# A planned TensorE order: keeping other matmuls out of the way of score groups

## The chip, the core and the metric

The kernel runs on one core of a Trainium2 chip. The metric is the device time of one execution in microseconds. The engines are TensorE (PE in the profile, PEld for its weight loads), VectorE (DVE), ScalarE (ACT), GpSimd (POOL) and SyncE (SP), which issues DMAs. Each works through its own list of instructions in order; semaphores tie the lists together.

## The reference

One transformer block with adaptive layer norm: 2048 tokens, width 640, 32 heads of 20, and a bilinear MLP of width 1536. Everything is bfloat16.

```python
def _A_ref(x, wqkv, wo):
    B, S, D = x.shape                       # 1, 2048, 640
    H = 32; Dh = D // H                     # heads of 20
    qkv = (x @ wqkv).reshape(B, S, 3, H, Dh).transpose(2, 0, 3, 1, 4)
    q, k, v = (qkv[0], qkv[1], qkv[2])
    scores = jnp.einsum('bhqd,bhkd->bhqk', q, k) * Dh ** (-0.5)
    p = _softmax(scores, axis=-1)
    o = jnp.einsum('bhqk,bhkd->bhqd', p, v)
    return o.transpose(0, 2, 1, 3).reshape(B, S, D) @ wo

def _B_ref(x, w_gate, w_up, w_down):
    g = jnp.einsum('bsd,df->bsf', x, w_gate)
    u = jnp.einsum('bsd,df->bsf', x, w_up)
    return jnp.einsum('bsf,fd->bsd', g * u, w_down)

mod = (_silu(c) @ w_mod).reshape(c.shape[0], 6, 1, -1)   # sa, ca, ga, sb, cb, gb
h = _layernorm(x) * (1 + ca) + sa
x = x + ga * _A_ref(h, A_wqkv, A_wo)
h = _layernorm(x) * (1 + cb) + sb
x = x + gb * _B_ref(h, B_w_gate, B_w_up, B_w_down)
```

The scores are 32 x 2048 x 2048 numbers, 134 million exponentials. Most are made by ScalarE's Exp. About a fifth of the score units go to VectorE instead, which makes an exponential out of integer steps (L1267, L1295, L1300 and L1303 below).

## The kernel before

The kernel doesn't write its instructions down in order. It makes tasks with durations and dependencies, and a planner in Python runs a small model of the five engines and decides, for each engine, which ready task comes next. What comes out is a fixed program. The lists of the engines are thus the result of the constants and of the picking rules.

The tensor that matters is `ps_all`, the eight accumulation banks of 512 float32 columns. Banks 0 to 2 and 3 to 4 are the two score buffers A and B, 5, 6 (and 2 at first) take everything else in turn (`G`), bank 7 collects the products with V.

A score group is two units of 128 keys x 512 queries (three in A late in the kernel: 1536 columns). ScalarE turns a group into the probabilities `PP` with one Exp; then its banks are free again. With the exponential of A running, TensorE is to fill B, and the other way round:

```python
    for g, (us, b0) in enumerate(glist):
        bset = setA if b0 == 0 else setB
        # ... ems: the score matmuls (L1209: ps_all<-QT,KT)
        ts = Task("pe", 216.0, ems, list(dict.fromkeys(deps)), ctr="pes", mode="S", name=f"S{g}")
        ts.acq = [(bset, "b", 1)]
        # ...
            ta = Task("act", nu * 512 / 1.2 + 52.0, fexp, [ts], prio=g, name=f"E{g}")   # L1243: PP<-ps_all
            ta.acq = [(pPs[g % 2], "p", nu)]

            def on_e(task, ...):
                bset.done(0, task)      # the exponential gives the score bank back
                sc.progress = max(sc.progress, g + 1)
```

All other TensorE work, projections, transposes, output projection and MLP, stands in "rounds" that take one bank of `G`. A matmul of these and the products with V are cut into quarters: four matmuls of 32 output rows side by side (mode "P"), which together take one step. Score groups are cut by rows (mode "S"), transposes use the whole array (mode "X"). A change of mode is planned as 100 ns:

```python
PE_SWITCH = 100.0
    def mode_start(mode, t):
        s = max(t, sc.pe_end)
        if sc.pe_mode is not None and sc.pe_mode != mode:
            s += PE_SWITCH
        return s
```

When TensorE is free in the model, `pick_pe` chooses. A score group whose bank is free comes first; else V products (`pv_issue`), if enough of them are ready; else the next matmul of a round (`pick_x`); else a filler, a matmul with the identity that only keeps TensorE active, when its activity of late is too low:

```python
    def pick_pe(t):
        sc.pull("pe")
        g = pvstate["sidx"]
        if g < NG:
            ts, us = score_q[g]
            if (...) and acquire_ready(ts, t):
                start = mode_start("S", t)
                rows = {}
                # ...
                d_attach(ts, t, apos[g] + EAGER, rows, 2, False)   # units for VectorE go along
                # ... issue the group
                return True
        # ... units for VectorE that are late
        if sc.recent(t) < FILL_MIN and ring() >= RINGLOW and pick_x(t, True):
            return True
        # ...
        cands = pv_candidates(t, PVCAP)
        it = st_pv["item"]
        if cands:
            info = item_info[it]
            ring_low = ring() < RINGLOW
            ending = info["left"] <= len(cands)
            force = ring_low or ending
            cands = pv_balance(cands, force)
            nwork = sum(1 if k == "a" else 4 for k, _ in cands)
            if cands and (nwork >= (PVMIN if just_s[0] else PVMAX) or force):
                just_s[0] = False
                pv_issue(cands, t)
                return True
        # ...
        if pick_x(t):
            return True
        # ...
        if t > 4000 and fill_ok(t, fill_deps):
            return do_fill(t)
        return False
```

A V product batch can hold up to 16 units, several steps. A filler is one matmul over the whole array (`FILL_MODE = 'X'`, 128x512 from `ident`). How early the rounds of the MLP and of the projections become pickable is set by gates in terms of finished exponentials (`GATE_F`, `K_LEAD`, `WM_NEED` and others).

The units for VectorE: L1267 evicts a unit to `DB` with an add and a maximum, L1295, L1300 and L1303 make two terms of four units in `DSS`, which go into V products as well. Lines of the profile that recur: L773 quarter matmuls of values, output projection and MLP, L888 and L940 those of K and Q, L1689 V products, L1936 fillers.

Of the kernel before, what the change touches and what calls it, by code (L numbers as in the profile page):

```python
# [23 lines left out]
DMA_LAT = 1700.0  # L24
STEAL_END = 85877.564
STEAL_GAP = 300.0
HAM_W = 3413.3
# [3 lines left out]
class Task:  # L31
    __slots__ = ("eng", "dur", "lat", "deps", "emits", "ctr", "prio", "gate", "acq", "on_start", "slots",
                 "start", "done", "needed", "val", "know", "nleft", "ready", "users", "name", "mode", "seq", "rt", "sem",
                 "nbytes", "cond", "alt", "land")

    def __init__(self, eng, dur, emits, deps=(), ctr=None, prio=0.0, lat=None, gate=0, acq=(), on_start=None,
                 name="", mode="X", nbytes=0):
        self.eng = eng
        self.dur = dur
        self.emits = emits if isinstance(emits, list) else [emits]  # L40
        self.deps = [d for d in deps if d is not None]
        self.ctr = ctr or eng
        self.prio = prio
        self.gate = gate
        self.acq = list(acq)
        self.on_start = on_start
        self.slots = {}
        self.start = None
        self.done = None
        self.needed = False  # L50
        self.val = None
        self.know = None
        self.name = name
        self.mode = mode
        self.users = []
        self.nbytes = nbytes
        self.sem = None
        self.cond = None
        self.alt = None
        self.land = 0.0  # L60
        if lat is None:
            lat = {"pe": PE_DRAIN, "act": ACT_LAT, "dve": DVE_LAT, "pool": 60.0}.get(eng, 0.0)
        self.lat = lat
# [50 lines left out]
class Sched:  # L114

    def __init__(self):
# [19 lines left out]
        self.ndup = 0  # L136
        self.nsteal = 0
        self.hist = []
        self.acts = []
        self.left = 0  # L140

    def add(self, task):
# [79 lines left out]
    def step_engine(self, eng):  # L222
# [5 lines left out]
        for k, task in enumerate(rl):  # L228
            if task.gate > self.progress or (task.cond is not None and not task.cond()):
                continue  # L230
            if self.acquire(task, self.t):
                rl.pop(k)
                self.finish_issue(task, self.t, task.dur)
                self.free_at[eng] = self.t + task.dur
                return True
# [168 lines left out]
HEADG = 600  # L404
EAGER = 0
X_POOL, X_PIECES, POOL_NS = 0, 4, 2.2
GU_ONE = 0
# [3 lines left out]
NPS = 4  # L411
TS_4X, TT_2X = 600.0, 1145.0
WM_GATE = 15
WM_NEED = 1.824
K_DIRECT = (0, 1, 2, 3)
Q_DIRECT = 2
K_LEAD = 0.703
K_ALL = (0,)
KD_LEAD = 0.686
DMA_WINDOW = 900000  # L420
D_LATE = 13
D_RES = 75
PVMIN, PVMAX, PVCAP = 2, 13, 16
GATE_F = [0.8, 0.788, 1.0, 0.673, 1.0]
FILL_MIN = 4200.0
FILL_HARD = 0.0
FILL_MODE = 'X'
DUP_MIN = 0.0
XN_POOL = ()
XFIRST = 0  # L430
LN2P = 1.495
NALT = 1
OPFIRST = 0
HT_L = 0.099
V_L = 0.079
LATE_A = 1.127
LATE_L = 3
LATEQ = (3,)
LATEQ_A = 0
LATEQ_F = 0.561  # L440
# [12 lines left out]
def build_kernel(nc, A_x, A_wqkv, A_wo, B_x, B_w_gate, B_w_up, B_w_down, c, w_mod, out):  # L453
# [96 lines left out]

    PPs = [alloc("PP", [128, NPS, w * 512], BF16) for w in (3, 2)]
    wo7 = alloc("wo7", [128, D], BF16)
# [99 lines left out]
    def pool(dur, f, deps=(), prio=3.0, **k):  # L652
        return sc.add(Task("pool", dur, f, deps, prio=prio, **k))

# [165 lines left out]
    def ln1(tc, prio):  # L820
# [3 lines left out]
        for i in range(4):  # L824
            t = tc * 4 + i
            bns = []
            for hf in range(2):
# [13 lines left out]
            if tc in XN_POOL:  # L841
                t_xn[tc].append(pool(1000, f, [p2] + dps, prio=prio + .5))
            else:
                t_xn[tc].append(dve(360, f, [p2] + dps, prio=prio + .05 + .1 * i))

# [344 lines left out]
    for k in range(KD):  # L1190
        t_wo.append(dve(395, lambda e, k=k: e.tensor_tensor(wo_sb[:, k, :], wo_sb[:, k, :], gab[:, 0, :], ALU.mult),
                         d_wo + ev_ga, prio=2.45))
# [3 lines left out]
    for f_ in range(FT):  # L1196
        t_wd.append(dve(395, lambda e, f_=f_: e.tensor_tensor(wd_sb[:, f_, :], wd_sb[:, f_, :], gab[:, 1, :],
                                                                ALU.mult), [d_wd] + ev_gb, prio=2.45))
# [19 lines left out]
    st_pv = {"item": 0, "free": [d_pz]}  # L1218
    d_state = {}
    for qi, (it, us) in enumerate(dquads):  # L1220
        d_state[qi] = {"units": us, "p1": [None] * 4, "slot": None, "item": it}
        for x, u in enumerate(us):
            u.quad = (qi, x)
# [50 lines left out]
    for qi, (it, us) in enumerate(dquads):  # L1274
# [3 lines left out]
        def term(f, deps, dur, name, slot=None, src=None, last=False, it=it, qi=qi, st_=st_):  # L1278
            t = Task("dve", dur, f, deps, prio=2.5 + .001 * qi, name=f"{name}.{qi}")
            if slot is not None:  # L1280
                t.acq = [(sSS, "s", 1)]
            t.cond = lambda: it <= st_pv["item"]

            def on_t(task):
                if slot is not None:
                    st_["ss"][slot] = task.slots["s"]
                if last:
                    sB0.done(st_["slot"], task)
# [16 lines left out]
        tm = term(fm, list(st_["p1"]), TS_4X, "M", slot=0)  # L1305
        if X_POOL and qi % X_POOL == 0:
            deps = [tm]
            for x in range(X_PIECES):
                w = 2048 // X_PIECES

                def fxp(e, x=x, w=w, st_=st_):
                    d = DSS[:, st_["ss"][0], x * w:x * w + w].bitcast(BF16)
                    return e.tensor_tensor(d, DB0[:, st_["slot"], x * w:x * w + w].bitcast(BF16), d, ALU.mult)
                t = Task("pool", w * POOL_NS + 150.0, fxp, deps, prio=.1 * qi, name=f"XP.{qi}")

                def on_p(task, x=x, st_=st_):
                    if x == X_PIECES - 1:
                        sB0.done(st_["slot"], task)
                        st_["src"][0] = [task]
                t.on_start = on_p  # L1320
                sc.add(t)
                deps = [t]
        else:
            term(fx, [tm], TT_2X, "X", src=0, last=True)
        term(fe, list(st_["p1"]), TS_4X, "EX", slot=1, src=1, last=True)

# [33 lines left out]
    def item_end_tasks(it):  # L1360
# [15 lines left out]
        else:  # L1376
            t3 = dve(sb_cost(n, 1.04), f3, [t2], prio=1.5)
        t4 = dve(n * 1.1 + 65, lambda e: e.transpose(OcT[:, cell["s"], 0:n], OTn[:, 0:n]), [t3], prio=1.5)  # L1378
# [32 lines left out]
    def suffix(ci):  # L1411
# [30 lines left out]
        for tl in range(ntl):  # L1442
# [21 lines left out]
            for hf in range(2):  # L1464
# [6 lines left out]
                      [p1], prio=1)  # L1471
            t_xn2.append(dve(360, lambda e, t=t, tl=tl: e.tensor_scalar(
                xn2[:, tl, :], xck[:, tl, :], mv2[:, t, 0:1], rs2[:, t:t + 1], op0=ALU.subtract, op1=ALU.mult),
# [153 lines left out]
    def mode_start(mode, t):  # L1627
        s = max(t, sc.pe_end)
        if sc.pe_mode is not None and sc.pe_mode != mode:
            s += PE_SWITCH  # L1630
        return s

# [204 lines left out]
    def pick_pe(t):  # L1837
# [44 lines left out]
        elif not tail_added[0]:  # L1882
# [6 lines left out]
            else:  # L1889
                tail_added[0] = False  # L1890
        if sc.recent(t) < FILL_MIN and ring() >= RINGLOW and pick_x(t, True):
            return True
# [9 lines left out]
        if cands:  # L1902
            info = item_info[it]
            ring_low = ring() < RINGLOW
            ending = info["left"] <= len(cands)
            force = ring_low or ending
            cands = pv_balance(cands, force)
            nwork = sum(1 if k == "a" else 4 for k, _ in cands)
# [102 lines left out]
```

The softmax here doesn't subtract the row's maximum and nothing guards it: scores larger than these inputs give would overflow.

## Time and profile before

| | before |
|---|---|
| time, median of 3 runs (lowest to highest) | 839.69 us (839.03 to 841.29) |
| span of the profiled execution | 836.0 us |
| TensorE clock granted, mean | 0.996 |
| Exp on ScalarE (L1243) | 778 instructions, 765.0 us |
| score matmuls (L1209) | 2560 instructions |
| VectorE score units (L1267) | 404 instructions, 267.0 us |
| fillers (L1936) | 119 instructions, 42.7 us |
| POOL busy | 78.5 us |

The span is what the profiler saw from first to last instruction. The record of a group of instructions reads: line, engine, operation, output from input, shapes, count, then busy time, mean length of one, idle time of the engine just ahead of them and what ended most of it. Two things need care. The end of a matmul is modelled, so a step of 216 ns shows as 385. And the records of consecutive exponentials overlap, so busy time says less than the distance between starts. In all text, a step is one pass of 512 columns through the array: four quarter matmuls or one whole one.

### The profile page before, as it was taken

To read this page: it belongs to the slowest core of one execution; us is meant where nothing else is said; L and a number is where in the kernel's file an instruction comes from. 1 tells how busy PE (TensorE), PEld (TensorE's weight loads), DVE (VectorE), ACT (ScalarE), POOL (GpSimd) and SP (SyncE) were. 2 spreads that over 40 slices of the span, in tenths; PEclk is the share of its full clock that TensorE was granted. 3 is DMA by queue.
4 is the path that set the end of the run, shared out by engine and by line. 5 is a ranking of instruction groups with operands and counts; after the bars stand their busy time and mean duration, and the time that the engine had idled before them with its cause. 6 is when DMAs were issued, how large, how long until landed. Compare 5 with 4: busy or idle time off the path is not lost.

```text
span 836.0 us, 28503 instructions
## 1 busy us (share of the span) xinstructions
PE 807.9 (97%) x12313; PEld 305.5 (37%) x12313; DVE 732.2 (88%) x1286; ACT 780.7 (93%) x809; POOL 78.5 (9%) x104
## 2 busy tenths in 40 slices
PE   8999999999999999999999999999999999999998
PEld 4433333222232222233232222332244433454577
DVE  7988999999799999998999999998789978757673
ACT  4899999999999999999999999999999999999921
POOL 2310000000011000000021000000011000001000
PEclk9999999999999999999999999999999999999999
DMA  9263411134200235000300221001200226106330
GB/s 301 74 192 88 95 43 43 49 98 126 58 18 20 58 79 160 2 15 20 92 2 13 53 60 39 13 22 40 53 4 22 53 60 130 45 29 141 84 82 20
DMA packets 115899, 54.29 MB, mean 65 GB/s; under 512 B 83771, under 2 KB 115775, under 8 KB 115775
## 3 DMA queue, kind: packets, MB, share of 16 engines
q1 hardware_dynamic: 114847, 51.33, 24.2%
q8 instruction: 97, 1.59, 0.8%
q10 hardware_dynamic: 928, 1.15, 0.4%
q14 instruction: 27, 0.22, 0.1%
HBM read 41.75 MB, written 8.41 MB: 60 GB/s over the span
## 4 chain that ended last, share of the span: by engine, by line
PE 63%; DVE 18%; ACT 13%; issue 5%; POOL 1%; DVEq 0%; ACTq 0%
PE ps_all L773 21%; PE ps_all L1209 20%; PE ps_all L1689 14%; ACT PP L1243 13%; DVE DB L1267 6%; PE ps_all L940 4%; DVE DSS L1300 2%; DVE DSS L1303 2%; DVE st L828 1%; PE ps_all L888 1%; DVE DSS L1295 1%; DVE OT L1366 1%; PE ps_all L1936 1%; POOL OTn L1371 1%; DVE OcT L1378 1%
## 5 line engine op out<-in xcount | busy, mean ns | idle before, releaser
L1243 ACT ACTIVATE PP<-ps_all 128x1024 bf16<-128x1024 f32 (+1 forms) x778 | 765.0, 1104 | 6.2 <-PE ps_all L1209 4.3
L1209 PE MATMUL ps_all<-QT,KT 32*128 32x512 bf16 (+1 forms) x2560 | 319.7, 340 | 12.4 <-ACT PP L1243 7.8
L1267 DVE TENSOR_SCALAR DB<-ps_all 128x512 int16<-128x512 f32 x404 | 267.0, 680 | 42.9 <-PE ps_all L1209 41.4
L1209 PEld LDWEIGHTS ps_all<-QT,KT 32*128 32x128 bf16 x2560 | 84.8, 91 | 264.1 <-ACT PP L1243 192.8
L1689 PE MATMUL ps_all<-PP,Vf 128*32 128x512 bf16 (+3 forms) x2076 | 161.5, 343 | 0.5 <-DVE OT L1366 0.4
L1300 DVE TENSOR_TENSOR DSS<-DB,DSS 128x2048 bf16<-128x2048 bf16 x101 | 122.0, 1208 | 0.0
L773 PE MATMUL ps_all<-h2T,stg 128*32 128x512 bf16 x1440 | 114.3, 386 | 1.2 <-DVE DB L1267 1.0
L1371 POOL TENSOR_TENSOR OTn<-OT,invT 128x512 bf16<-128x512 f32 (+1 forms) x39 | 48.0, 1232 | 612.3 <-DVE invT L1369 612.3
L1689 PE MATMUL ps_all<-DSS,Vf 128*32 128x512 bf16 (+1 forms) x968 | 79.6, 349 | 1.1 <-DVE DSS L1300 0.5
L1689 PEld LDWEIGHTS ps_all<-PP,Vf 128*32 128x32 bf16 (+1 forms) x2076 | 46.2, 94 | 86.1 <-issue 78.7
L1303 DVE TENSOR_SCALAR DSS<-DB 128x2048 int16<-128x2048 int16 x101 | 71.9, 712 | 0.0
L1295 DVE TENSOR_SCALAR DSS<-DB 128x2048 int16<-128x2048 int16 x101 | 69.4, 687 | 0.9
L773 PE MATMUL ps_all<-wd,hprod 128*32 128x320 bf16 x1152 | 57.9, 301 | 0.2 <-DVE DB L1267 0.2
L773 PEld LDWEIGHTS ps_all<-h2T,stg 128*32 128x32 bf16 x1440 | 31.7, 95 | 37.0 <-issue 20.5
L1936 PE MATMUL ps_all<-ident 128*128 128x512 bf16 x119 | 42.7, 409 | 1.9 <-POOL ident L729 1.5
L1558 DVE CAST gsb<-ps_all 128x512 bf16<-128x512 f32 (+1 forms) x48 | 29.5, 614 | 7.5 <-PE ps_all L773 7.2
L773 PE MATMUL ps_all<-wo,Ocp 128*32 128x320 bf16 x640 | 34.0, 301 | 0.9 <-DVE OcT L1378 0.5
L1689 PEld LDWEIGHTS ps_all<-DSS,Vf 128*32 128x32 bf16 x968 | 24.5, 95 | 27.4 <-issue 11.9
L773 PEld LDWEIGHTS ps_all<-wd,hprod 128*32 128x32 bf16 x1152 | 27.5, 96 | 17.8 <-issue 8.5
L773 PE MATMUL ps_all<-wV,hT 128*32 128x320 bf16 x640 | 31.5, 301 | 0.1
L1366 DVE STREAM_TRANSPOSE OT<-ps_all 128x512 f32<-128x512 f32 (+1 forms) x40 | 24.1, 603 | 7.6 <-PE ps_all L1689 7.5
L940 PE MATMUL ps_all<-hT,wq 128*32 128x512 bf16 x375 | 30.4, 382 | 0.0
(109 smaller groups left out, 507.7 us busy)
## 6 DMA issues: line engine op xcount, KB each, us to landing
stg<-in_B_w_gate_dram SPq DMA_DIRECT2D x50, 160.0 KB
stg<-in_B_w_up_dram SPq DMA_DIRECT2D x50, 160.0 KB
QT<-q_rows SPq DMA_DIRECT2D x22, 128.0 KB
KT<-k_rows SPq DMA_DIRECT2D x84, 32.0 KB
wm<-in_w_mod_dram SPq DMA_DIRECT2D x3, 800.0 KB
x<-in_A_x_dram SPq DMA_DIRECT2D x7, 320.0 KB
xck<-in_A_x_dram SPq DMA_DIRECT2D x3, 640.0 KB
wd<-in_B_w_down_dram SPq DMA_DIRECT2D x1, 1920.0 KB
```

The source lines that it names most:

```text
L773: return lambda e, b: e.matmul(ps[32 * x:32 * x + 32, b, c0:c0 + n], lhs()[:, 32 * x:32 * x + 32], rhs(), tile_position=(0, 32 * x), start ...
L940: f = [lambda e, b_, k=k, x=x: e.matmul(ps[x:x + min(32, w - x), b_, :], wx[:, k, r0 + x:r0 + min(x + 32, w)], hT[tc][:, k, :], tile_posit ...
L1209: ems.append(lambda e, i=i, kt=kt: e.matmul(dstf()[:, i * u.n:(i + 1) * u.n], KT[32 * u.s:32 * u.s + 32, u.j, kt * 128:(kt + 1) * 128], QT ...
L1243: return e.activation(PPs[g % 2][:, cellp["p"], 0:nu * 512], ps[:, b0:b0 + nu, :].rearrange("p b c -> p (b c)"), AFT.Exp, scale=ESCALE)
L1267: return e.tensor_scalar(DB0[:, st_["slot"], x * 512:(x + 1) * 512], bank(cell["b"]), EBIAS, 0.0, op0=ALU.add, op1=ALU.max)
L1295: return e.tensor_scalar(DSS[:, st_["ss"][0], :], DB0[:, st_["slot"], :], 0x7F, 0x3F00, op0=ALU.bitwise_and, op1=ALU.bitwise_or)
L1300: return e.tensor_tensor(d, DB0[:, st_["slot"], :].bitcast(BF16), d, ALU.mult)
L1303: return e.tensor_scalar(DSS[:, st_["ss"][1], :], DB0[:, st_["slot"], :], 0x7F80, 2, op0=ALU.bitwise_and, op1=ALU.bitwise_or)
L1366: t1 = Task("dve", n * 1.1 + 70, lambda e: e.transpose(OT[:, 0:n], ps[:, BPV, 0:n]), [], prio=0.0, name=f"T1.{it}")
L1371: f3 = lambda e: e.tensor_tensor(OTn[:, 0:n].rearrange("p (b c) -> p b c", c=32), OT[:, 0:n].rearrange("p (b c) -> p b c", c=32), invT[:, ...
L1689: ems.append(lambda e, i=i, kt=kt, stt=stt, stp=stp: e.matmul(ps[32 * s:32 * s + mc, BPV, 0:u.n], Vf[:, (kt * H + 4 * u.j + s) * VW:(kt * ...
L1936: task.emits = [lambda e: e.matmul(ps[:, b_, :].rearrange("p (a b) -> p a b", a=4), ident[:], idb)]
```

## The change

The planner learns when the next score group can start (`s_ready`: its bank is given back and its inputs are there). If that is at most `HOLD` = 110 ns away, TensorE is left free in the plan, and nothing else begins. A V product batch is cut so that it ends at most `PVTOL` = 300 ns after that moment. A switch of mode is counted from the end of the last matmul, so that it is free when TensorE has been idle. Fillers after the first score group are made of quarters, which stay in mode P. Units for VectorE may go along with score groups three units earlier (`EAGER`), and their terms may be made ahead by one item (`TAHEAD`). Tasks of VectorE and GpSimd marked `lk` are no longer planned at the same time. Then the gates and thresholds are fitted anew. The arithmetic is the same. The diff, cut:

```diff
-STEAL_END = 85877.564
-STEAL_GAP = 300.0
+STEAL_END = 66197.894
+STEAL_GAP = 188.158
@@ class Sched
+    def locked(self, eng, task):
+        if not task.lk:
+            return False
+        if self.lk_end["pool" if eng == "dve" else "dve"] > self.t:
+            return True
+        ...
@@ step_engine
+            if self.locked(eng, task):
+                continue
             if self.acquire(task, self.t):
                 rl.pop(k)
+                self.lock(eng, task)
@@ constants
-EAGER = 0
-X_POOL, X_PIECES, POOL_NS = 0, 4, 2.2
+EAGER = 3
+X_POOL, X_PIECES, POOL_NS = 0, 4, 1.95
+HOLD = 110
+PVTOL = 300
+TAHEAD = 1
-WM_NEED = 1.824
+WM_NEED = 1.798
-K_LEAD = 0.703
+K_LEAD = 0.642
-KD_LEAD = 0.686
+KD_LEAD = 0.704
-D_LATE = 13
+D_LATE = 12
-PVMIN, PVMAX, PVCAP = 2, 13, 16
-GATE_F = [0.8, 0.788, 1.0, 0.673, 1.0]
+PVMIN, PVMAX, PVCAP = 2, 11, 16
+GATE_F = [0.8, 0.869, 0.999, 0.673, 1.0]
-FILL_MODE = 'X'
+FILL_MODE = 'P'
-LN2P = 1.495
+LN2P = 1.539
-V_L = 0.079
+V_L = 0
-LATEQ_A = 0
+LATEQ_A = 2
@@ the terms of VectorE units
-            t.cond = lambda: it <= st_pv["item"]
+            t.cond = lambda: it <= st_pv["item"] or (it == st_pv["item"] + 1 and tleft.get(it - 1, 0) == 0 and TAHEAD)
@@ mode_start
-        s = max(t, sc.pe_end)
         if sc.pe_mode is not None and sc.pe_mode != mode:
-            s += PE_SWITCH
-        return s
+            return max(t, sc.pe_end + PE_SWITCH)
+        return max(t, sc.pe_end)
+
+    def s_ready():
+        g = pvstate["sidx"]
+        if g >= NG:
+            return None
+        ts, us = score_q[g]
+        r = 0.0
+        for d in ts.deps:
+            if d.done is None:
+                return None
+            r = max(r, d.done + SEM)
+        for pool, key, refs in ts.acq:
+            a = pool.avail()
+            if a is None:
+                return None
+            r = max(r, a[0])
+        return r
@@ pick_pe
+        sr = s_ready()
+        if HOLD and sr is not None and t < sr <= t + HOLD and ring() >= RINGLOW:
+            return False
         if sc.recent(t) < FILL_MIN and ring() >= RINGLOW and pick_x(t, True):
             return True
...
             force = ring_low or ending
+            if PVTOL and sr is not None and not force:
+                k = int((sr + PVTOL - mode_start("P", t)) // 216.0)
+                if k < 1:
+                    cands = []
+                else:
+                    ...     # at most k units for each of the four quarters
+                    cands = aa
+        if cands:
             cands = pv_balance(cands, force)
```

Code for moving one of the VectorE terms to GpSimd (`X_POOL`) and the layer norm there (`LN_POOL`) comes in too, but both are off.

## The prediction

> **What bounds the kernel now.** I read the busy shares first, then stretches of the span, then the exponentials by shape, then who waits for whom, then the order in time of a few microseconds. Part 1 of the page:
>
> ```profile
> PE 807.9 (97%) x12313; PEld 305.5 (37%) x12313; DVE 732.2 (88%) x1286; ACT 780.7 (93%) x809; POOL 78.5 (9%) x104
> ```
>
> TensorE (PE) and ScalarE (ACT) are both nearly always busy, and the ends of matmuls are modelled, so this line alone doesn't choose. The stretches do (columns: stretch, length, then busy us and instructions of PE, PEld, DVE, ACT, POOL, granted clock, DMA share, GB/s):
>
> ```profile
> 0.00:17.50 17.50, 13.60 (x162) 7.15 (x166) 12.91 (x52) 5.02 (x9) 3.96 (x13) 0.90 0.96 300
> ...
> 468.00:542.00 74.00, 73.47 (x960) 21.36 (x956) 71.17 (x110) 73.28 (x78) 5.49 (x4) 1.00 0.17 40
> ...
> 675.30:678.70 3.40, 3.34 (x32) 0.72 (x32) 2.71 (x5) 2.75 (x3) 0.00 (x0) 0.50 0.04 9
> 798.90:836.00 37.10, 33.04 (x1056) 28.22 (x1054) 18.35 (x49) 4.49 (x13) 1.23 (x2) 1.00 0.13 35
> ```
>
> The first exponential starts at 17.5 us and the last at 798.3, so head and tail are 17.5 and 37 us, and in between ACT is busy practically all the time. But busy isn't full speed. The groups by shape:
>
> ```profile
> L1243 ACT ACTIVATE PP<-ps_all 128x1024 bf16<-128x1024 f32 x688 | 656.1, 1054 | 4.7 <-PE ps_all L1209 3.0
> L1243 ACT ACTIVATE PP<-ps_all 128x1536 bf16<-128x1536 f32 x89 | 132.7, 1490 | 1.5 <-PE ps_all L1209 1.3
> ```
>
> Consecutive exponentials overlap in the record (the single ones have a median length of 1026 and 1460 ns), so the cost of one is the distance from its start to the next start. Taken over the trace, the lowest tenth of these distances is 903 ns for 1024 elements and 1330 ns for 1536. With these as floor the exponentials need 739.6 us; from first to last start they take 780.8. The excess is 41.2 us, and it is all that a better order can win. I cut it into ten equal parts by number of exponentials. The first (17.5 to 101 us, projections and ScalarE evictions between) has 14.9 us. The nine others have 26.3: 100 distances lie 80 to 180 ns over the floor and sum to 12.4; 20 lie more than 180 over it and sum to 6.8; the other 7.1 is jitter of some 10 ns each.
>
> The class of 100 has one picture, seen in the order in time (start, length, engine, line; ACT does eight exponentials in 7.81 us here, 976 ns each):
>
> ```profile
> 476.37 7.81 ACT L1243 ACTIVATE PP<-ps_all 128x1024 bf16<-128x1024 f32 x8
> ...
> 477.90 0.39 PE L1209 MATMUL ps_all<-QT,KT 32*128 32x512 bf16 x2
> ...
> 478.21 0.40 PE L1689 MATMUL ps_all<-PP,Vf 128*32 128x512 bf16 x4
> ...
> 478.44 0.39 PE L1689 MATMUL ps_all<-DSS,Vf 128*32 128x512 bf16 x4
> ...
> 478.76 0.39 PE L1209 MATMUL ps_all<-QT,KT 32*128 32x512 bf16 x2
> ...
> 479.08 0.83 PE L773 MATMUL ps_all<-h2T,stg 128*32 128x512 bf16 x12
> ...
> 479.85 0.39 PE L1209 MATMUL ps_all<-QT,KT 32*128 32x512 bf16 x3
> ```
>
> L1209 is a score group. Between the first two lie two steps of four quarter matmuls, between the next two lie three (x12). Score starts are 0.86 and then 1.09 us apart, and the pattern repeats: 1.95 us a pair, where two exponentials need 1.81. From a score group's start to its exponential's start 429 ns pass at best, so a score group may start up to about 375 ns after the recorded end of the exponential that frees its bank; in the trace, groups 200 to 300 ns late have 14 ns of mean excess, 300 to 500 ns late 46, 500 to 1000 late 222. Of the 419 that are 300 to 1000 ns late, 356 have a step of a projection or of the MLP right ahead of them, the others V products or fillers. TensorE is the bound in dense stretches, ScalarE in thin ones. The wait list puts only 7.8 us on score groups waiting for ScalarE, because in dense stretches nobody is seen waiting: both are "busy".
>
> **What the Trainium skill says.** TensorE: Matmul & The Clock Gate, Part 3, The mechanism: matmuls start and end in program order; so a score group can't overtake a step already issued. The trace agrees: the score group at 479.85 starts 0.77 us after the run of twelve began, three steps and a switch, though its bank had been free before. TensorEngine Tiling, Key Properties: changing the tiling mode drains the array. Here start to start is 217 ns inside a mode and 312 to 315 ns across score/quarter boundaries at 512 columns, so about 97 ns a switch. ScalarE: Activation LUTs, What ACT_TABLE_LOAD costs: 0.833 ns per element for every function; here (1330-903)/512 = 0.834, so the floor can't fall. TensorE: Matmul & The Clock Gate, Part 1, What's actually happening: the clock falls to half rate after a window of 3.4 us in which TensorE did too little. The trace has one such window in mid-kernel (675.3 to 678.7, clock 0.50), and exponentials 0.80, 0.43 and 0.21 us over the floor stand in and right behind it.
>
> **The change part by part.** Instruction counts of the built programs tell what the plan does; no kernel operation is added or removed besides fillers.
> - Work done: 688+89+1 exponentials, 404 VectorE score units and all products are the same. Evictions that ScalarE takes from VectorE in the head change: two more of Vf and one more of hT, one fewer each of QT, KT and KPA; by their rows 2x425 + 782 - 687 - 585 - 585 = -225 ns, nothing that counts.
> - Fillers: 119 full-array ones become 19, plus 248 quarter ones, four to a step, so 62: 81 steps, 38 fewer x 216 ns = 8.2 us of TensorE time. They stood in thin stretches, so alone they win nothing.
> - Switches: mode runs in the order fall from 1621 to 1548: 73 x about 97 ns = 7.1 us of TensorE time, mostly because quarter fillers no longer leave the mode.
> - Density, which is the point. Counting work between score groups in steps of 512 columns, fillers included, in the stretch of two-wide groups (tenths 2 to 7 by score work): before 480 gaps, 92 with three or more steps, 152 adjacent pairs of gaps with five or more in sum; after 472, 54 and 93. By tenth, steps before are 178, 156, 182, 152, 162, 180 and after 164, 160, 165, 153, 159, 164. A gap of k steps takes 0.315+0.217(k-1)+0.312 us: 0.84 for two, 1.06 for three. Nine hundred and three ns hold 2.27 steps at most, so 80 gaps hold 182: tenths 2, 4 and 7 were at the limit before, and none is after. The work goes into the thin tenths, where fillers had stood. In runs of ten gaps, 25 of 48 had 21.9 steps or more, 14 of 47 after.
> - Worth: pairs of five or more steps fall by 39%, full runs of ten by 44%. An isolated pair costs nothing (375 ns of slack), so the loss falls faster than the count; I choose 60% of the 12.4 us: 7.4. Of the 6.8 in longer ones, some are a score block held by VectorE units or an eviction, which EAGER=3 and the earlier terms ease: I choose 1.5.
> - Head: the same stages; after the first score group the gaps of over four steps hold about 89 steps after against 78 before: 11 x 0.217 = 2.4 us worse; against that all gaps but the first hold 225 against 232, and there are 8 gaps of three instead of 14. Taken as 0 with 2.5 us either way.
> - Tail: steps after the last score group 154.5 against 152.5: +0.4 us.
> Sum: -7.4 - 1.5 + 0 + 0.4 = -8.5. Time 839.7 - 8.5 = 831.2 us.
>
> **Rivals.** (a) VectorE becomes the limit: 88% busy, 71.2 of 74 us in the dense stretch, and its 404 units at 680 ns hold the spare score banks. With TensorE on time, ACT asks 7% more of VectorE in exactly those stretches. Against it: only 2.0 us of score waits are put on DB. It would give back half: 835 to 836. (b) The plan's clock is not the chip's: it counts on 216 ns steps and a fixed 100 ns switch, and holds on the strength of a release that it foresees to 110 ns. Then holding costs idle TensorE without score groups coming sooner, and work is pushed to the end: 838 to 842. Against it: the order itself is thinner, whatever the clock. (c) Fewer fillers let the clock fall in more windows; the one above cost 1.4 us, so two more make 834. (d) Almost all of the excess after the head goes, 20 us: 820. Against: 7.1 of 26.3 are jitter.
>
> **Range and chances.** (a) to (c) lie 3 to 10 us above the sum, (d) 11 below; the uncertain share (40 to 85% of 12.4) is 3 us and the head 2.5. Eight in ten: 824 to 838. Two per cent faster is below 822.9, needs 17 us of the 41: 0.07. Slower than 856.5 needs a plan that breaks: 0.02.
>
> **What would show it.** Distances 80 to 180 over the floor after the head: 100 should fall to about 40, their sum to 5 us; score starts in dense stretches 0.86 to 0.91 apart instead of alternating 0.86 and 1.08; the ACT groups' means 1054 to about 1045; spans of head and tail within 2.5 us of 17.5 and 37; the half-rate window near 675 gone or alone. Wrong if the sum of this class stays over 9 us though the order has fewer three-step gaps, or if the tail or the first 100 us move by more than 3.

## The result and the profile after

| | before | after |
|---|---|---|
| time, median (lowest to highest) | 839.56 us (839.03 to 841.29), 4 runs | 829.95 us (829.19 to 832.08), 4 runs |
| span of the profiled execution | 836.0 us | 830.3 us |
| first exponential starts | 17.5 us | 19.1 us |
| last exponential starts | 798.3 us | 792.6 us |
| from there to the end | 37.7 us | 37.7 us |
| distances over the floor, in all | 41.2 us | 33.9 us |

The ratio of after to before is 0.9886, with an interval of 0.9863 to 0.9909: 1.1% faster. 831.2 us were predicted.

Part 1 of the page after has every engine's busy time a little lower or the same, and shares of the span that barely moved:

```profile
PE 799.2 (96%) x12461; PEld 299.9 (36%) x12461; DVE 731.8 (88%) x1286; ACT 770.3 (93%) x809; POOL 75.2 (9%) x104
```

ScalarE's busy time fell by 10 us with the same 778 exponentials. The groups by shape show how little busy time says here (columns as before: busy us, mean ns, idle before):

```profile
L1306 ACT ACTIVATE PP<-ps_all 128x1024 bf16<-128x1024 f32 x688 | 648.1, 1107 | 9.2 <-PE ps_all L1270 7.5 <-PE ps_all L1788 1.4
L1306 ACT ACTIVATE PP<-ps_all 128x1536 bf16<-128x1536 f32 x89 | 134.2, 1507 | 0.2
```

The mean record of a 1024-wide exponential grew from 1054 to 1107 ns, while the mean distance from start to start fell from 961 to 951. The distance is the cost. The order in time of a dense stretch, the same program stage as the one shown before the change:

```profile
475.26 9.39 ACT L1306 ACTIVATE PP<-ps_all 128x1024 bf16<-128x1024 f32 x10
...
476.48 0.39 PE L1270 MATMUL ps_all<-QT,KT 32*128 32x512 bf16 x3
476.80 0.40 PE L1788 MATMUL ps_all<-PP,Vf 128*32 128x512 bf16 x4
477.03 0.39 PE L814 MATMUL ps_all<-h2T,stg 128*32 128x512 bf16 x4
477.38 0.39 PE L1270 MATMUL ps_all<-QT,KT 32*128 32x512 bf16 x2
...
477.69 0.61 PE L814 MATMUL ps_all<-h2T,stg 128*32 128x512 bf16 x8
...
478.29 0.39 PE L1270 MATMUL ps_all<-QT,KT 32*128 32x512 bf16 x3
478.61 0.40 PE L1788 MATMUL ps_all<-PP,Vf 128*32 128x512 bf16 x4
...
478.84 0.60 PE L814 MATMUL ps_all<-h2T,stg 128*32 128x512 bf16 x8
...
479.38 0.39 PE L1270 MATMUL ps_all<-QT,KT 32*128 32x512 bf16 x3
```

Score groups (L1270) start 0.90, 0.91 and 1.09 us apart: two steps, two, then three. A gap of three steps still occurs, but no longer every second time, and the ten exponentials take 9.39 us, 939 ns each where it was 976. Over the whole trace, 425 of 776 score groups started over 300 ns after the recorded end of the exponential that frees their bank; now 156 do, and the median went from 317 to 187 ns. The list of waits has TensorE now seen waiting more often for ScalarE (us in total, times, longest):

```profile
PE ps_all L1270 <- ACT PP L1306: 10.5, 36, 0.6
...
PE ps_all L1270 <- DMA QT<-q_rows: 1.8, 1, 1.8
```

Before it was 7.8 us in 25 waits. The second line is a disturbance of this one execution. The stretch from 101 to 110 us has it (stretch, length, PE, PEld, DVE, ACT, POOL busy, clock, DMA share, GB/s):

```profile
0.00:19.06 19.06, 14.30 (x166) 7.17 (x170) 13.44 (x55) 5.50 (x9) 4.67 (x14) 0.91 0.98 305
462.00:536.00 74.00, 73.04 (x883) 19.68 (x881) 73.58 (x113) 73.04 (x80) 5.69 (x4) 1.00 0.20 45
101.00:110.00 9.00, 7.17 (x84) 1.85 (x76) 4.27 (x7) 6.02 (x7) 0.00 (x0) 0.81 0.24 68
792.60:830.30 37.70, 34.26 (x1094) 28.93 (x1086) 19.39 (x50) 5.01 (x14) 1.23 (x2) 1.00 0.15 41
```

TensorE waited 1.8 us for a block of Q, and then the clock was at half rate for 3.4 us. The profiled execution is the slowest of the four (832.08 us); the other three had spans of 827.4 to 828.2 us and higher mean clocks (0.998 to 1.000 against 0.996). The profiled execution of the kernel before is in turn faster than the others: it took 838.12 us, where the lowest of the four is 839.03. So the two profiles understate the gain from both sides: 5.7 us in the spans, 9.6 in the medians.

Where the 5.7 us of the two profiles come from: start of the first exponential +1.6, excess in the first tenth of the exponentials +2.0 (14.9 to 16.9), excess in the nine others -9.4 (26.3 to 16.9), end 0.0. Each of the two profiles has one half-rate stretch in these nine parts (before at 675 us, after at 105 us), and each is worth 1.4 us of excess, so they cancel. The wait for Q is in the first tenth, 1.8 us of its +2.0.

### The profile page after: what moved, and what is told of

It reads as the page before. It is cut to its first block, busy times and chain, and to the rows that moved or that the text cites. A ratio compares the mean times of both kernels' runs of the same rounds, so it can differ in the third digit from the quotient of the medians.

```text
span 830.3 us, 28806 instructions
## 1 busy us (share of the span) xinstructions
PE 799.2 (96%) x12461; PEld 299.9 (36%) x12461; DVE 731.8 (88%) x1286; ACT 770.3 (93%) x809; POOL 75.2 (9%) x104
## 4 chain that ended last, share of the span: by engine, by line
PE 51%; ACT 30%; DVE 11%; issue 7%; DMA 1%; SPq 0%; ACTq 0%; DVEq 0%
ACT PP L1306 30%; PE ps_all L814 17%; PE ps_all L1270 16%; PE ps_all L1788 12%; DVE DB L1330 4%; PE ps_all L1001 3%; DVE DSS L1367 2%; PE ps_all L949 1%; DVE DSS L1370 1%; DVE DSS L1362 1%; DMA QT<-q_rows 1%; DVE OT L1449 1%; PE ps_all L828 0%; DVE st L889 0%; PE ps_all L2054 0%
## 5 line engine op out<-in xcount | busy, mean ns | idle before, releaser
L1306 ACT ACTIVATE PP<-ps_all 128x1024 bf16<-128x1024 f32 (+1 forms) x778 | 755.0, 1152 | 9.3 <-PE ps_all L1270 7.5
L1270 PE MATMUL ps_all<-QT,KT 32*128 32x512 bf16 (+1 forms) x2560 | 321.6, 340 | 17.0 <-ACT PP L1306 10.5
L1330 DVE TENSOR_SCALAR DB<-ps_all 128x512 int16<-128x512 f32 x404 | 266.6, 679 | 37.9 <-PE ps_all L1270 36.9
L1270 PEld LDWEIGHTS ps_all<-QT,KT 32*128 32x128 bf16 x2560 | 85.5, 91 | 281.8 <-ACT PP L1306 241.9
L1367 DVE TENSOR_TENSOR DSS<-DB,DSS 128x2048 bf16<-128x2048 bf16 x101 | 125.4, 1241 | 0.0
L1454 POOL TENSOR_TENSOR OTn<-OT,invT 128x512 bf16<-128x512 f32 (+1 forms) x39 | 43.6, 1117 | 620.5 <-DVE invT L1452 592.5
L1362 DVE TENSOR_SCALAR DSS<-DB 128x2048 int16<-128x2048 int16 x101 | 68.7, 680 | 0.8
L1370 DVE TENSOR_SCALAR DSS<-DB 128x2048 int16<-128x2048 int16 x101 | 69.2, 685 | 0.0
L814 PE MATMUL ps_all<-wo,Ocp 128*32 128x320 bf16 x640 | 33.9, 301 | 0.5 <-DVE xck L1538 0.2
L1652 DVE TENSOR_TENSOR hprod<-ps_all,gsb 128x512 bf16<-128x512 f32 x36 | 24.4, 678 | 3.5 <-PE ps_all L814 3.4
```

What stands on the lines that cost most here:

```text
L814: return lambda e, b: e.matmul(ps[32 * x:32 * x + 32, b, c0:c0 + n], lhs()[:, 32 * x:32 * x + 32], rhs(), tile_position=(0, 32 * x), start ...
L1270: ems.append(lambda e, i=i, kt=kt: e.matmul(dstf()[:, i * u.n:(i + 1) * u.n], KT[32 * u.s:32 * u.s + 32, u.j, kt * 128:(kt + 1) * 128], QT ...
L1306: return e.activation(PPs[g % 2][:, cellp["p"], 0:nu * 512], ps[:, b0:b0 + nu, :].rearrange("p b c -> p (b c)"), AFT.Exp, scale=ESCALE)
L1330: return e.tensor_scalar(DB0[:, st_["slot"], x * 512:(x + 1) * 512], bank(cell["b"]), EBIAS, 0.0, op0=ALU.add, op1=ALU.max)
L1362: return e.tensor_scalar(DSS[:, st_["ss"][0], :], DB0[:, st_["slot"], :], 0x7F, 0x3F00, op0=ALU.bitwise_and, op1=ALU.bitwise_or)
L1367: return e.tensor_tensor(d, DB0[:, st_["slot"], :].bitcast(BF16), d, ALU.mult)
```

## The experiments

Each kernel was profiled once and timed beside the kernel before. All sums below use the same floors, 903 and 1330 ns, and the same nine tenths, the 77th exponential and later. "Class" is the sum of excess in distances that lie 80 to 180 ns over the floor, with their number. "Dense pairs" are adjacent gaps with five or more steps in sum, counted in the built order in the stretch of two-wide groups, as in the prediction. "Filler steps" counts the fillers in each trace, four quarters as one step. Ratios are to the kernel before timed beside it; for `rule_switch`, `pvtol_off` and `nofill_head`, which have four executions each, the medians alone give 0.990, 0.988 and 0.987, so their lower printed ratios do not make them faster than the changed kernel.

| kernel | dense pairs | filler steps | class, us (number) | over 180, us | first tenth, us | last exponential to end, us | time, us |
|---|---|---|---|---|---|---|---|
| before | 152 | 119 | 12.4 (100) | 6.8 | 14.9 | 37.7 | 839.6 |
| after | 93 | 81 | 2.9 (24) | 7.0 | 16.9 | 37.7 | 829.95 |
| hold_off | 163 | 136 | 12.7 (103) | 6.1 | 17.1 | 37.9 | 841.1 |
| switch_only | 170 | 136 | 14.3 (116) | 8.5 | 18.0 | 37.8 | 846.8 |
| rule_only | 31 | 55 | 2.1 (15) | 15.5 | 19.4 | 47.8 | 850.0 |
| rule_switch | 101 | 85 | 3.5 (27) | 6.2 | 15.5 | 38.5 | 831.6 |
| pvtol_off | 107 | 92 | 3.2 (26) | 5.2 | 15.2 | 37.9 | 829.7 |
| hold_60 | 131 | 113 | 7.1 (65) | 3.2 | 16.2 | 40.0 | 834.2 |

**Which part of the change is it?** First the hold alone taken away:

```diff
-HOLD = 110
+HOLD = 0
```

> The changed kernel with HOLD = 0, everything else as changed (the refitted constants, the cut V batches, quarter fillers, EAGER, TAHEAD). In its order the stretch of two-wide groups has 108 gaps with three or more steps and 163 pairs of gaps with five or more (92 and 152 before the change, 54 and 93 after). Theory (holding thins the dense stretches, and that is the gain): the class of distances 80 to 180 ns over the floor is back at 11 to 14 us, the time at 837 to 842 us. Rival (the refitted constants bring the gain): the time stays at 829 to 832 us and the class at 3 us.

Measured: 841.09 us (839.6 to 843.99), ratio to the kernel before 0.9994 (0.9969 to 1.0018). The class is at 12.7 us. All of the gain is gone, with every refitted constant, the quarter fillers, EAGER and the cut V batches still there. The old picture is back in its order in time:

```profile
477.24 0.39 PE L1270 MATMUL ps_all<-QT,KT 32*128 32x512 bf16 x2
...
477.56 0.40 PE L1788 MATMUL ps_all<-PP,Vf 128*32 128x512 bf16 x4
477.79 0.39 PE L814 MATMUL ps_all<-h2T,stg 128*32 128x512 bf16 x4
...
478.11 0.39 PE L1270 MATMUL ps_all<-QT,KT 32*128 32x512 bf16 x2
478.43 0.40 PE L1788 MATMUL ps_all<-DSS,Vf 128*32 128x512 bf16 x4
478.65 0.61 PE L814 MATMUL ps_all<-h2T,stg 128*32 128x512 bf16 x8
...
479.19 0.39 PE L1270 MATMUL ps_all<-QT,KT 32*128 32x512 bf16 x4
```

0.87 with two steps, 1.08 with three. The saved switches of mode, which the prediction put at 7.1 us of TensorE time, are not the gain either: the order changes mode 1621 times before, 1548 times in the changed kernel and 1554 times here.

Then the other way round: the kernel before, with the rules put in and all its constants kept.

```diff
+HOLD = 110
+PVTOL = 300
 def mode_start(mode, t):
-    s = max(t, sc.pe_end)
     if sc.pe_mode is not None and sc.pe_mode != mode:
-        s += PE_SWITCH
-    return s
+        return max(t, sc.pe_end + PE_SWITCH)
+    return max(t, sc.pe_end)
+# s_ready, the hold in pick_pe and the cut of V batches as in the change
```

> The kernel before with three things only: HOLD = 110, PVTOL = 300, and a switch of mode counted from the end of the last matmul. All constants, fillers over the whole array, EAGER = 0 as before. In its order 68 gaps have three or more steps, 101 pairs have five or more, and 155.0 steps stand behind the last score group. Theory: class of 80 to 180 at 3 to 5 us, time 830 to 833 us, so nearly the whole gain without any refit. Rival (refit): 836 to 840 us.

Measured: 831.56 us (829.85 to 838.97), ratio 0.9876 (0.9794 to 0.9959, four executions and a wide interval). The class is at 3.5 us. With the constants of before, fillers over the whole array and EAGER = 0, the median is 8.4 us under the kernel before timed beside it, where the changed kernel has 9.6. The refit is not what brings the gain; whether it adds the last 1.2 us can't be told with this spread.

**What the two rules do, each alone.** The hold and the cut without the new count of a switch:

```diff
+HOLD = 110
+PVTOL = 300
 # mode_start as before: 100 ns are charged after idle time too
```

> The kernel before with HOLD = 110 and PVTOL = 300 only; a switch of mode is still charged after idle time, as before. In its order 29 gaps have three or more steps, 31 pairs five or more, but 193.2 steps stand behind the last score group, against 152.5. Theory (two ends of one budget: what is held back in the middle must be done at the end): class of 80 to 180 at 2 us or less, the last exponential starts 12 to 18 us earlier than before, and the time from there to the end is 40.7 x 0.217 = 8.8 us longer, 46 to 47 us; time 830 to 836 us. Rival (only the start of score groups matters): the end stays at 37.7 us and the time is 825 us or less.

Measured: 849.96 us (847.0 to 855.02), ratio 1.0108 (1.008 to 1.0136): slower than the kernel before, where 830 to 836 us were expected. The middle is thinner than in any other kernel, class 2.1 us. But the end grew by 10.1 us, from 37.7 to 47.8, where 8.8 were expected from 40.7 steps, and the last exponential starts at 798.3 us, not 12 to 18 us earlier. That part of the expectation fell: 8.9 us of excess stand between 105 and 184 us, 8.6 of them in 13 distances over 180 ns, and that is 6.1 us more than the same exponentials have in the kernel before. The waits of ScalarE there, between 140 and 172 us (total, times, longest):

```profile
ACT PP L1245 <- PE ps_all L1708: 5.2, 4, 2.4
ACT PP L1245 <- PE ps_all L1211: 0.8, 3, 0.4
```

L1708 is the V product in this kernel. The exponential does not wait for scores here, but for a place in `PP`, which V products have to empty. In the order in time, 37 quarter matmuls of the projection of values (L775) run in one lump from 161.40 to 162.98 us just ahead of the V products, and the exponential at 163.11 waited 2.4 us. I read this so: held back too often, the projection of values came when it could wait no longer. A hold moves work, and work has a date: at the end, or where the next stage needs it. The clock has a part in this loss that no run separates: beside the half-rate stretch of the start, this profile has stretches at 33.6, 84.8 and 477.4 us, and all executions of this kernel had mean clocks of 0.980 to 0.992.

The count of a switch without the hold:

```diff
 def mode_start(mode, t):
-    s = max(t, sc.pe_end)
     if sc.pe_mode is not None and sc.pe_mode != mode:
-        s += PE_SWITCH
-    return s
+        return max(t, sc.pe_end + PE_SWITCH)
+    return max(t, sc.pe_end)
```

> The kernel before with one thing: a switch of mode is counted from the end of the last matmul. Its order has 105 gaps of three or more steps and 170 pairs of five or more (before 92, 152), 136 fillers, 152.2 steps behind the last score group. Theory (this rule alone gains nothing; with the hold it is what lets work be done in the middle): class of 80 to 180 at 12 to 15 us, time 839 to 843 us. Rival (it is the real gain): 833 us or less.

Measured: 846.77 us (844.27 to 848.54), ratio 1.0073 (1.0056 to 1.009), class 14.3 us. The class is as expected, the time 4 us above the range: the first tenth has 3.1 us more than before and the waits over 180 ns 1.7 more. Neither rule alone gains anything; both together do. Between `rule_only` and `rule_switch` the count of a switch is the only difference, so the count is the cause of that loss. How it comes about is my reading of the planner and is not shown: with the old count it charged 100 ns for a switch after a hold, though the array had been idle, saw less time than there was, and pushed work away. `PVTOL` uses the same count, and no run tells which of the two rules suffered.

**The cut of V batches and the size of the hold.**

```diff
-PVTOL = 300
+PVTOL = 0
```

> The changed kernel with PVTOL = 0: V product batches are not cut. In its order 66 gaps have three or more steps, 107 pairs of gaps five or more (54 and 93 in the changed kernel, 108 and 163 without the hold); the steps behind the last score group are the same, 154.5. Theory (density by holding is the gain, the cut of V batches a small share of it): class of 80 to 180 at 3.5 to 5 us, time 830 to 833 us. Rival (the cut of V batches is half of the gain): 834 to 836 us.

Measured: 829.67 us (829.38 to 830.04), ratio 0.9823 (0.9747 to 0.9899), class 3.2 us, both just under the expected ranges. The cut of V batches brings nothing that can be measured here, though its order has 14 dense pairs more.

```diff
-HOLD = 110
+HOLD = 60
```

> The changed kernel with HOLD = 60 instead of 110. Its order has 76 gaps of three or more steps and 131 pairs of five or more, between the changed kernel (54, 93) and the one without hold (108, 163); fillers 113, steps behind the last score group 155. Theory (the gain goes with the number of dense pairs): class of 80 to 180 at 6 to 9 us, time 833 to 837 us. Rival (a threshold, not a dose): as with 110, 829.5 to 831 us, or as without, 840 to 842.

Measured: 834.17 us (832.35 to 836.1), ratio 0.9909 (0.9877 to 0.9941), class 7.1 us. Both in the expected range. The steps at the end were expected to take as long as before, and took 2.3 us longer (40.0 us, with TensorE busy 34.5 of them); 1.5 us of this are one wait of TensorE for `h2Tc` from VectorE, which the changed kernel doesn't have. With the others, this makes the relation of dense pairs and class plain: 170, 163, 152, 131, 107, 101, 93 and 31 pairs have 14.3, 12.7, 12.4, 7.1, 3.2, 3.5, 2.9 and 2.1 us. It falls steeply between 150 and 107 and is flat below.

**Are fillers the gain?** In the table, filler steps rise and fall nearly as the dense pairs do, so they are a rival: perhaps fewer fillers are the gain. The kernel before, its fillers behind the 60th us of the plan cut to 8 columns in their places:

```diff
+        if t > 60000:
+            task.emits = [lambda e: e.matmul(ps[:, b_, 0:8], ident[:], ident[:, 0:8])]
         sc.activity(start, 512.0)
```

> The kernel before with its fillers behind the 60th us cut to 8 columns instead of 512, in the same places of the same order. Theory (fillers stand where TensorE has time anyway): the class of 80 to 180 stays at 11 to 13 us and the time at 838 to 841 us, or more where the clock falls to half rate. Rival (the 38 fillers fewer are part of the gain): 831 to 835 us.

Measured: 884.89 us (871.44 to 892.03); the spread is too wide for a ratio. The profiled execution (892.03 us, the slowest of the four) had a mean clock of 0.885, with stretches at half rate of up to 41 us. One of them, in the same columns as above:

```profile
377.00:397.00 20.00, 20.00 (x165) 4.67 (x164) 14.00 (x21) 13.93 (x14) 0.00 (x0) 0.50 0.03 6
```

The loss of clock, 31 us even in the fastest execution, swamps the time, so the time alone doesn't answer the question. The distances do. Away from the half-rate stretches, 500 exponentials of the nine tenths can be set beside the same 500 of the kernel before: the class has 9.5 us in 78 distances with the small fillers, and 10.3 us in 83 with the full ones. Over the nine tenths it is 10.4 us (84), where 11 to 13 were expected. And of the class in the kernel before, only two distances have a filler in either of the two gaps ahead of the late score group. So fillers don't make the groups late. Their smaller number goes with the thinner order and is not what takes the class away.

Ahead of the first long stretch at half rate (203 us), the order in time with the small fillers, and then the same place in the kernel before:

```profile
201.30 0.39 PE L1209 MATMUL ps_all<-QT,KT 32*128 32x512 bf16 x2
201.62 0.40 PE L1689 MATMUL ps_all<-DSS,Vf 128*32 128x512 bf16 x4
201.95 0.18 PE L1942 MATMUL ps_all<-ident 128*128 128x8 bf16 x1
202.22 0.39 PE L1209 MATMUL ps_all<-QT,KT 32*128 32x512 bf16 x2
```

```profile
200.82 0.39 PE L1209 MATMUL ps_all<-QT,KT 32*128 32x512 bf16 x2
201.14 0.39 PE L1936 MATMUL ps_all<-ident 128*128 128x512 bf16 x1
201.45 0.40 PE L1689 MATMUL ps_all<-DSS,Vf 128*32 128x512 bf16 x4
201.79 0.40 PE L1209 MATMUL ps_all<-QT,KT 32*128 32x512 bf16 x4
```

From 185 to 203 us no two matmuls start more than 0.6 us apart, in either kernel. With the small fillers the clock falls, with the full ones it stays. What differs is the work of the four fillers from 199 to 203 us, 8 columns each instead of 512. The changed kernel has 38 filler steps less and keeps its clock, presumably since projection and MLP steps stand in their places; no run shows that reason.

**Is TensorE's time in the gaps really what counts, and has the changed kernel room?** Extra work without a new plan. First, score groups twice in the kernel before:

```diff
                 sc.finish_issue(ts, start, dur)
+                if 80 <= g < 580 and g % 8 == 0:
+                    ts.emits = ts.emits + ts.emits
```

> The kernel before with the score matmuls of every eighth group between groups 80 and 580 (63 groups, with their VectorE units) issued twice in a row into the same banks; the order is otherwise the same and the planner doesn't know. That is 63 x 0.217 = 13.7 us more TensorE work at the most, about 0.22 us at a time. Theory (score groups of the kernel before have no room left: 425 of 776 start over 300 ns after the release, and about 375 ns are free): some 40% of it is paid, 5 to 6 us, and the time is 844 to 847 us. Rival (only ScalarE's own rate counts): nothing is paid, 840 us.

And the same edit in the changed kernel:

> The same in the changed kernel, same groups, same extra work. Theory (the hold has given score groups room: 156 of 776 start over 300 ns after the release): 1 to 3 us are paid, the time is 831 to 833.5 us, and the extra of this pair is less than half that of the kernel before. Rival (TensorE is no less tight, only the order is luckier): the same 5 to 6 us as in the kernel before, 835 to 836 us.

Measured: 847.35 us (845.69 to 856.18), ratio 1.0079 (1.0048 to 1.0109), 7.6 us over the median of the kernel before timed beside it; and 838.18 us (837.08 to 841.34), ratio 0.9973 (0.9951 to 0.9995), 8.2 us over the 829.95 us of the changed kernel, which was not timed beside it. Both pay alike. Against my theory, but the experiment was also ill made: twice the matmuls make the score group itself 0.22 us longer, and its exponential waits for the second half. Taken apart by position behind the doubled group, exponential by exponential against the trace without doubling:

```
extra excess, mean ns     doubled  next  2nd  3rd
before                       149    20    3   -11
after                         99    27   11     3
lateness of the group, median ns, without and with
before               346/348   361/516   328/386   306/324
after                172/220   160/393   167/296   172/276
```

Most is paid at the doubled group. The next group starts late in both, and neither pays much for that: 20 and 27 ns.

So a second pair, with an extra step that makes no score group longer: the first step of a gate round twice, the second overwriting the first.

```diff
                     f = quarters(n, lambda k=k, cell=wbuf[w_]: cell["t"][:, k, :], lambda k=k: h2T[:, k, 0:n],
                                  k == 0, k == KD - 1)
+                    if k == 0 and w_ == 0 and n == 512:
+                        f = f + f
```

> The kernel before with the first step of each of the 36 gate rounds of 512 columns (MLP, first three query chunks) issued twice, the second overwriting the first: 36 x 0.217 = 7.8 us more TensorE work in gaps between score groups, and no score group is longer for it. The planner doesn't know, the order is otherwise the same. Theory (the dense stretches of the kernel before have no room): with a median lateness of 300 to 350 ns of 375 free, some 150 ns of each 217 are paid: 4.5 to 6.5 us, time 844 to 846 us. Rival (both orders are equally tight, as the doubled score groups seemed to say): before and after pay the same, 4 to 6 us each.

> The same 36 steps in the changed kernel. Theory: with a median lateness of 170 ns, an extra step is at or just over the free 375 and is worked off in the next gaps: 1 to 3 us are paid, time 831 to 833 us, at most half of what the kernel before pays. Rival (equally tight): 4 to 6 us, 834 to 836 us.

Measured: 845.29 us (842.22 to 860.88), ratio 1.005 (1.0027 to 1.0073), 5.1 us over the kernel before; and 834.25 us (832.71 to 839.55), ratio 0.9911 (0.9883 to 0.9938), 4.3 us over the same 829.95 us of the changed kernel. In the traces, the exponentials 150 to 640 have 5.1 and 3.6 us more excess than without the extra steps, of 7.8 us put in: 65% and 46%. But the first of these profiles has a half-rate stretch from 359.3 to 362.7 us, and 1.5 of the 5.1 us stand there. Without it 3.6 us are left, 47%. So both pay alike: the second time is above my 1 to 3 us and in the range of the rival, and the rival was right. TensorE's time in the gaps is on the path in both kernels, and the changed one shows no more room for a whole step. That fits the lengths: a gap of two steps takes 0.84 us of 0.903, so a step of 0.217 needs about four gaps to be worked off, and there are dense pairs on the way.

**The later start.**

```diff
-        if t > 4000 and fill_ok(t, fill_deps):
+        if t > 4000 and (pvstate["sidx"] or t < 9000) and fill_ok(t, fill_deps):
```

> The changed kernel without fillers between the 9th us of the plan and the first score group. In its trace five fillers at half clock stand from 10.13 to 12.22 us ahead of the transposes of the first chunk, one in the kernel before (10.17 to 10.55), and the first exponential starts at 19.06 instead of 17.48 us. Theory (these fillers delay the head by 1.6 us, because the transposes' inputs were there): first exponential at 17.3 to 17.7 us, time 828 to 829 us. Rival (the fillers stand where the transposes wait anyway, and the clock needs them): first exponential at 19 us or later, time 830 us or more.

Measured: 828.94 us (828.5 to 830.28), ratio 0.9817 (0.9741 to 0.9893), but the first exponential starts at 19.02 us, as in the changed kernel. The rival was right about the head; the 830 us or more that it expected did not come. TensorE's order of the first microseconds in this kernel:

```profile
10.80 2.32 PE L916 MATMUL ps_all<-ident,xn 128*128 128x128 bf16 x20 [0.61 <-DVE xn L900]
14.04 2.32 PE L949 MATMUL ps_all<-hT,wk 128*32 128x512 bf16 x20 [0.93 <-ACT hT L922]
16.15 1.55 PE L949 MATMUL ps_all<-hT,wq 128*32 128x512 bf16 x20
```

The transposes start 1.4 us earlier than in the changed kernel (12.22), but the clock is then at half rate from 9.9 to 16.7 us instead of 3.4 us, and the twenty K matmuls take 2.32 us instead of 1.26. The fillers cost as much as they save. The time is the lowest of all, 1.0 us under the changed kernel, with ranges that touch (829.19 is that one's lowest); I don't call it better.

## Why the prediction was right, and where it wasn't

The mechanism was the one named: gaps with too many steps made score groups late, and a thinner order ended that. `hold_off` and `rule_switch` show it from both sides. The terms of the sum came out as follows.

- **Density.** Class predicted to fall from 12.4 to 5 us and from 100 to about 40 distances; it fell to 2.9 and 24. The step was the one named, and its size was off: 77% instead of the 60% chosen. The table of dense pairs shows why: the class is nearly gone at 40% fewer pairs.
- **Waits over 180 ns.** Predicted -1.5 us by EAGER and the earlier terms; measured +0.2 in the profiles (6.8 to 7.0), and again +0.2 without the half-rate stretch that each of the two has (5.4 to 5.6). This step failed: they stayed. In `pvtol_off` and `nofill_head`, which keep EAGER and TAHEAD too, they are 5.2 and 5.7; `rule_switch` without both has 6.2.
- **Head.** Predicted 0 with 2.5 either way. The first exponential is 1.6 us later; the first tenth has 2.0 us more, of which 1.8 is the wait for Q at 104 us in this execution. nofill_head and pvtol_off, nearly the same order, have 15.0 and 15.2 in the first tenth, against 14.9 before. So +1.6 to +1.9 in these, in the range, and on the side of loss. In the profile itself the two together are +3.6, over the 3 us that I had named as a sign of being wrong; it is under 3 only if the wait for Q is set aside as a disturbance.
- **End.** Predicted +0.4, measured 0.0.
- **Sum.** -7.4 -1.5 +0 +0.4 was predicted; -9.5 +0.2 +3.6 +0.0 and -0.1 of jitter make the -5.7 of the profiles. The medians are 9.6 apart. With the 1.8 us of the wait for Q set aside, the terms give -7.6; the other 2.0 us can't be taken apart, for the two profiled executions are not the usual ones, as said above. That the prediction came within 1.3 us is partly luck: the gain in the class was taken too small, the waits and the head too kindly, and these errors lay on opposite sides.
- **Rivals.** VectorE as the limit (a): didn't come; its score units wait 36.9 us for TensorE against 41.4. The plan's clock (b): not in the changed kernel, but `rule_only` is a loss of this kind, with a switch charged at the wrong time. The clock (c): two extra windows were feared; one came, in the profiled execution, and the one near 675 us was gone. Nearly all excess gone (d): no, 16.9 of 26.3 us remain, 7.0 of them jitter.
- **A sign that I named wrongly.** I expected the mean record of an exponential to fall to about 1045 ns; it rose to 1107. The start-to-start distance is the measure, as I had said myself.
- **A slack that was a little wide.** The prediction gave a score group about 375 ns after the recorded end of the exponential that frees its bank. Its own figures give less: two beats of 903 ns, minus a record of 1026 and the 429 from group to exponential, are 351.
- **A window named loosely.** The stretch from 675.3 to 678.7 us is the one at half rate. The one with little work lies just ahead of it (671.9 to 675.3, TensorE busy 2.81 of 3.40 us); in the half-rate stretch TensorE is busy 3.34 of 3.40.
- **A reason that was too broad.** I said that after the change no tenth is at TensorE's limit. By the average of steps that is so, but an extra step still costs 46% of its length; the room is in pieces smaller than a step.

What stays open: why the waits over 180 ns stay at 5 to 7 us, what share of the loss of `rule_only` is the clock, and what brings the half-rate stretches that come in single executions.

## What to carry to other kernels

When an in-order engine feeds a buffer that another engine frees on a fixed beat, count its work between two releases in whole steps: work that exceeds the beat on average must be moved to where fillers or idle time stand, and a rule that leaves the engine free just ahead of a release does that. Such a rule only pays if the planner has the costs right around the idle time (here a switch charged after idle time stood between 1.0% of gain and 1.1% of loss), and if the moved work isn't due somewhere else. Test a bundle by taking out its rules one at a time: here one rule and the count of a switch were the gain, and the refit of a dozen constants was not. And look at the clock of a profile before its sums are used: one stretch of 3.4 us at half rate was worth 1.4 to 1.5 us here, as much as the difference that the extra steps seemed to show.

## What the runs showed of the hardware that I had not expected

- Records of exponentials get longer when ScalarE is fed in time: 337 of 688 of the 1024-wide ones are over 1100 ns in the changed kernel and 94 in the one before, while the median distance from start to start is 904 against 920. The records overlap more; their sum is no measure.
- With fillers of 8 columns instead of 512, the clock fell to half rate for stretches of up to 41 us with TensorE shown busy without a pause, and beforehand with no two matmul starts more than 0.6 us apart. 31 to 52 us of this kernel's time hang on fillers that compute nothing. The Trainium skill, TensorE: Matmul & The Clock Gate, HAM oscillation — how this bites in real kernels, puts the rule in the abstract as no idle gaps over some 3.4 us. The `small_fill` run fell without one: from 185 to 203 us TensorE is shown busy for 17.42 of 18 us, and for 17.77 in the kernel before, which keeps its clock there. So what the fillers do counts, and not only the gaps between starts; how much work is enough was not measured.
